# Fused H3 convolution and Infini-attention: bound products in four column tiles, a first butterfly on VectorE for two channel blocks, two loads on another queue, and a new stored order

## The chip, the cores and the metric

The kernel runs on one NeuronCore of a Trainium2 chip. A core has five engines that run side by side: TensorE (PE, matrix products into PSUM), ScalarE (ACT), VectorE (DVE), GpSimd (POOL) and SyncE (SP), the last used here only to issue DMAs. Each works through its own instructions in order; semaphores hold an instruction until what it needs is done. The metric is device time in microseconds of one execution. Before the change the median of seven runs is 310.45 us (308.61 to 312.26).

## The reference

Two independent computations are set beside each other in the last axis of the output, [1, 2048, 1280] in bf16. S = 2048, D = 640, H = 32 heads of 20.

```python
# A: long convolution (H3)
k_shift = sum over t of k shifted down by t rows * shift_k[:, t]     # t = 0..3
kv = k_shift * v
y  = irfft(rfft(kv, 2S) * rfft(ssm_k, 2S))[:S]                     # causal convolution over S
A  = q * (y + kv * ssm_D)
# B: segment attention with a memory (N = 4 segments of L = 512, per head)
for s in range(N):
    p = softmax(qs @ ks.T * scale + causal_mask)
    a_mem = (phi(qs) @ M) / (phi(qs) @ z + 1e-6)                   # phi(t) = t+1 if t > 0 else exp(t)
    o_s = g * a_mem + (1 - g) * (p @ vs)                           # g = sigmoid(beta)
    M += phi(ks).T @ vs;  z += sum(phi(ks))
B = concat(o_s) @ wo                                               # q, k, v = x @ wq, x @ wk, x @ wv
out = concatenate([A, B], -1)
```

## The kernel before

**Part A** goes through five blocks of 128 channels (`dp` 0 to 4). For each block the transform of length 4096 is split into four residues of time (`c` = 0..3), each a product with a cosine and sine table. Stages, in `a_chunks`:
- `load_kv` brings v (`vt`, four DMAs of 128 KB) and k transposed (`kr`); `load_sk` brings ssm_k and transposes it to `kT`; `load_q` brings q. For block 0 v is issued on ScalarE's queue, for the others on GpSimd's.
- `kshift(b)` forms the shifted k as 16 small products into a PSUM bank, and VectorE multiplies it with v in place (`vt<-w,vt`).
- `fwd(kind, c)` multiplies `vt` (kind "X") or `kT` (kind "K") with the table `Wf` into two banks, and ScalarE copies each to `F`.
- `bfly(kind)` combines the four residues on VectorE into `Xh` or `Kh`.
- `pointwise`, `ybfly` multiply the spectra (`S`) and combine them back, and `inverse(c)` makes four output tiles with the table `Wi`, multiplied with q by VectorE (`outa`) and stored by a DMA on GpSimd's queue.

A residue transform has eight products of 128x256. When a kind is in `SUMMED` (before: "X" for every block), `fwd` computes for c = 0..3 the sums and differences of two residues at once, by accumulating 16 products instead of eight, the difference with a negated table `Wfn`. `bfly` then skips its first two VectorE operations, one addition and one subtraction of [128, 2048].

**Part B** has eight units, u = 2 s + half: a segment s and a half of 16 heads. `proj(t)` projects k, q and v for 128 tokens (15 products of 128x320, three copies by ScalarE), and a DMA transpose on SP brings k and q to `KQT` with the head dimension on partitions, 32 partitions a head. `bound` finds for every query an upper bound of its scores, so that the softmax needs no maximum: VectorE takes the largest absolute value of each k dimension (`kam`, 128x2048 to 128x4), multiplies a selection table by it (`A`), takes |q| (`qabs`), and TensorE sums over a head's 20 dimensions. Four products, one for each group g of four heads, accumulate in 16 rows of one bank; ScalarE copies them to `bT`, and four small DMAs on SP put them into row 20 of each head's block in `KQT`, where k has ones. `mem` updates the memory. `attn(g)` makes scores for four heads at once in four row tiles, always in the one buffer `st` of four PSUM banks; ScalarE exponentiates them to `ET`, TensorE multiplies with v and the memory, and VectorE normalises. `outt` and `outproj` project to the output.

All other products use the four banks "w". The pool of banks, the tile buffers (most exist once, so the next user waits for the last reader) and the data dependencies are tracked by a recorder. Operations are first recorded, in program order, then emitted in the order that `ORDER` lists, a compressed list of operation numbers. That order alone decides how the parts A and B are interleaved on each engine and each DMA queue. DMAs issued on SP, ScalarE and GpSimd queue behind each other per issuer. Line 216 is the emission, so nearly every instruction in the profile has that line: groups are told apart by tile names.

The identity (`ident`, 32 KB) turns x into `xT` for the first segment and builds `skd`; before the change it is the second DMA of ScalarE's queue, behind x.

Of the kernel before, what the change touches and what calls it, by code (L numbers as in the profile page):

```python
# [12 lines left out]
BF16_NP = ml_dtypes.bfloat16  # L13
bf16 = mybir.dt.bfloat16
f32 = mybir.dt.float32
i16 = mybir.dt.int16
ALU = mybir.AluOpType
# [4 lines left out]
S = 2048; D = 640; C = 512; P = 1024  # L22
# [21 lines left out]
def small_consts():  # L44
    p = np.arange(128)
    d = p % 32
    hl = p // 32
    sel = np.zeros((128, 4, 16), np.float32)
    for g in range(4):
        ok = d < DH  # L50
        sel[p[ok], g, 4 * hl[ok] + g] = -1.0
    maskbd = np.zeros((128, 4, VW), np.float32)
    epsrow = np.zeros((128, 4), np.float32)
    for hh in range(4):
        rows = (hl == hh) & (d < DH)
        maskbd[rows, hh, 0:DH + 1] = 1.0
        epsrow[32 * hh + DH + 1, hh] = EPS
    later = np.zeros((128, 5, 128), np.float32)
    for b in range(4):
        later[:, b] = np.where(np.arange(128)[None, :] <= 32 * b + p[:, None] % 32, 0.0, -1e9)  # L60
    later[p, 4, p % 32] = 1.0
    return sel.astype(BF16_NP), maskbd.astype(BF16_NP), epsrow, later.astype(BF16_NP)
# [213 lines left out]
class K3:  # L276
    def __init__(self, ctx, tc, A_q, A_k, A_v, A_shift_k, A_ssm_k, A_ssm_D, B_x, B_wq, B_wk, B_wv, B_wo, B_beta, out):
# [48 lines left out]
        }  # L326
        self.skw = c.tile([128, 5, 4], bf16, name="skw")
        nc.gpsimd.dma_start(out=self.skw[:], in_=self.shift_k.rearrange("(c p) t -> p c t", p=128))
        self.ident = const("ident", np.eye(128).astype(BF16_NP), bf16, nc.scalar)
        bt = self.bt = c.tile([128, H], bf16, name="bt")  # L330
        nc.gpsimd.dma_start(out=bt[:], in_=B_beta.partition_broadcast(128))
        self.sel = const("sel", sel_np, bf16)
# [48 lines left out]
    def a_chunks(self, dp):  # L381
# [16 lines left out]
        def load_kv():  # L398
            vt = st["vt"] = self.ring("vt", [128, 4, 4, 128])
            for b in range(4):  # L400
                (nc.gpsimd if dp else nc.scalar).dma_start(out=vt[:, b], in_=self.v[512 * b:512 * b + 512, dsl].rearrange("(p c) d -> p c d", c=4))
            kr = st["kr"] = self.ring("kr", [128, 1, 4, KPAD + 512])
            nc.gpsimd.memset(kr[:, 0, :, 0:KPAD], 0.0)
            for c in range(4):
                nc.sync.dma_start_transpose(out=kr[:, 0, c, KPAD:KPAD + 512], in_=self.k[:, dsl].rearrange("(r c) d -> r d c", c=4)[:, :, c])
            w1 = st["skd"] = self.ring("skd", [128, 4, 128])[:]
            V.tensor_tensor(out=w1, in0=self.ident[:, None, :].to_broadcast([128, 4, 128]), in1=self.skw[:, dp, :, None].to_broadcast([128, 4, 128]), op=ALU.mult)
# [18 lines left out]
        def fwd(kind, c):  # L426
            def f():
                if c == 0:
                    st["F"] = self.ring("F", [128, 4, 2, 512])
                F = st["F"]  # L430
                terms = [(c, Wf[:, :, c, :])]
                if kind in SUMMED:
                    p = c % 2
                    terms = [(p, Wf[:, :, p, :]), (p + 2, (Wf[:, :, p + 2, :], self.Wfn[:, :, p, :])[c // 2])]
                for i in range(2):
                    pf = self.bank("w")
                    for j in range(2):
                        o = pf[:, 256 * j:256 * j + 256]
                        last = kind == "K" and i == 0 and terms[0][0] == 0
                        mms = [(w[:, h, 256 * i + 128 * j:256 * i + 128 * j + 128], st["vt"][:, h:4:2, cc, :] if kind == "X" else st["kT"][:, cc, h:4:2, :])  # L440
                               for cc, w in terms for h in range(2)]
                        for n, (w, rhs) in enumerate(mms):
                            nc.tensor.matmul(o, lhsT=w, rhs=rhs, start=(n == 0), stop=(n == len(mms) - 1 and not last))
                        if last:
                            nc.tensor.matmul(pf[:, 256 * j:256 * j + 128], lhsT=self.ones[0:1, :], rhs=st["Drow"][:], start=False, stop=True)
                    nc.scalar.copy(out=F[:, c, i, :], in_=pf)
            return f

        def bfly(kind):
            def f():  # L450
                F = st["F"]
                X = st[kind] = self.ring(kind + "h", [128, 8, 512])
                T = F[:, 0:2]
                if kind not in SUMMED:
                    T = X[:, 1:8:2, :].rearrange("p (c i) r -> p c i r", c=2)
                    V.tensor_tensor(out=T, in0=F[:, 0:2], in1=F[:, 2:4], op=ALU.add)
                    V.tensor_tensor(out=F[:, 2:4], in0=F[:, 0:2], in1=F[:, 2:4], op=ALU.subtract)
# [62 lines left out]
    def b_proj_chunks(self, u):  # L520
# [43 lines left out]
        def bound():  # L564
            kam = self.ring("kam", [128, 4], f32)
            V.tensor_reduce(out=kam[:], in_=KQT[:, 0:4, :], axis=AX.X, op=ALU.max, apply_absolute_value=True)
            A = self.ring("A", [128, 4, 16])
            V.tensor_tensor(out=A[:], in0=self.sel[:], in1=kam[:, :, None].to_broadcast([128, 4, 16]), op=ALU.mult)
            if s > 0:
                nc.scalar.activation(out=PqT[:], in_=QT, func=ACTF.Exp)  # L570
                tq = self.ring("tq", [128, 4, L])
# [3 lines left out]
            V.tensor_scalar(out=qabs[:].bitcast(i16), in0=QT.bitcast(i16), scalar1=0x7fff, scalar2=None, op0=ALU.bitwise_and)  # L575
            pb = self.bank("w")
            for g in range(4):
                nc.tensor.matmul(pb[0:16, :], lhsT=A[:, g, :], rhs=qabs[:, g, :], start=(g == 0), stop=(g == 3))
            bT = self.ring("bT", [16, L])
            nc.scalar.copy(out=bT[:], in_=pb[0:16, :])  # L580
            for hl in range(4):
                r = 32 * hl + DH
                nc.sync.dma_start(out=KQT[r:r + 1, 4:8, :], in_=bT[4 * hl:4 * hl + 4, :])

        def mem():
            src, dst = self.Mbd[half][s % 2], self.Mbd[half][(s + 1) % 2]
# [101 lines left out]


BANKS = {"st": (1, 2048), "w": (4, 512)}  # L690
SUMMED = ("X",)
ORDER = (
    'c-jTQ0{|FQ6a~<G-@AXdZQHhO+qT)v8f&)g)lgdvHP*b^YPP+aJ13G6iI5Ok5DAW0h=C}GhNy@DASNOrpaKlh5g9^Ei)xWAw#7zV#6dKRZkdo7Q7n$duvnHDDJ_*Hw-grNQXw7^SX_%|'
    'nJtMWwPY3_=`4$7w7izpGFdiDiPT7M8LTSOBB!N8LQ8FFERp4~+?L<cT4Kv%`K*BDvNXtmLRQ#{SUF38@>ao;pqKTwtjKN!EeCQUAM&H34YZ<G+=^Kt<U(!~K~WUOSSx@bRuJPX53->='
    '@**jQ*>D?b$xs=UP!Uzo$NE|sl(3RE-ul@@%Z@=d*hX1@D~94Ii4quXlWe+uWixGpl|?y}vC>w`%Gv-MVbxFr-&$#mv2Uz8zP3762enWW=}{N8F~w$}6zbXxn`+Z+q}{X0cE_gRu6<|s'
    'Z5pOxI;vPzYlTK=jY`%Sm8}h0pe<UW8LC-zn`Jeu2^v^aG_(e&X${dFEvz0|+82Y@$1AI6_3e|*wOW=DwQaV|vpLot9ncOB?4d2Q<+j4++eA#pc6^O)_y$`s39qf0HMh^!$llljYh??q'
    'wLP-N*1;azTkD9G)(f4{2|X|ybI``xT1R_soopta*<xE{OKhoqhbGq4Uf4@(XYK7<^u{bi^v>4B<|2}Jwf7d;qxd}ZL?67s2m5H-@Xp+y;W?svay-QjJV6Sqv9-1oE3wL!VHH-}a?Hm9'
    'tiW2-^mVolwS2v8u*SX^du*e{^(Bxu@r788Zr0uQ+BRE*MTqV3JdSU&%@*Gic<>(9(>7rv`l25q_<C%>7R2=a7>EJbZci+sSNDCE$p5t(zTckOe-_oF`Hz;&lXzlJ>O1im578C((FG6i'
    '2yqyT-9i7!_QQNHe#Fn%VLPp%e~(7~vmL}Qb_hdozz$kkkKyV3KfFUM-;F(Zji0a&Z?MIFKypvvL-7)?u+?_q7aYK0r1Vt&y`}fJ$lyQNA^R8ge3$)--FDd8`bU7j+9$MgvbBFkcmK_5'
    'u&y7mFBpNNcFa<H4{zgX{J3@X+Ws3h;|Px7DC&D{jzj}*=`H+(owQay2%SAP>v%WM;q5)6=k%VQ$+LNL@94d}lXvjUJ{Vm*i}&@@$nFt148L10Z|dhPBKvr5Z|1%In4h-lJnny3EuONP'  # L700
    'JmDw(ycP9gKG4tDSsRXi-rq<0Xdj2d9*KE8uMhG8KG=tNJ|E-xy@*F<887QY{dYg*!@QvX;iGX1<1q$f{eu62LVn5r^vizQ%Xx9X<t6+tFYmX#g5PlCd9Ua<eYk(+BYlLQ^D7>g_k5C<'
    '^oxGYvwA7N>ZSd<pFshi?3Mh9SN5mwyzkTfk<ak=c<dkWouBc)eU{Jkv;L2N>*5`M;Z^)B&f$SS^r~LXqw)gI<07IkunH@2EH2n_Ou+A`%&M%$Q8<BK{0b*A&hPqo&#gRq=6O|I&pn@J'
    '`vjlkFTI5R^#-iN|NM==^|?OJ=ld&f$Y`v~iJpjw`Oc&By%$w6t@e0K!+K1?HJ+9!xz-zTo!94UZ_GdO!9RL@e(md>`o{l)$u-5N`Uc<V3w)FRgU!Chr375)30X*sJQ<TS6|YzlrsfqC'
    'RuRSIRV$;U?9FL@3F(-g8F<rf*(Zm-ctLIDXWzoo+RRPt%f)`(F4~{=m(^AsU9uat#LH``SI{zV!lsO)xLWSb*qr$ll#zd<tTHnO%V~vI(@J0ETRjuEc`jZ?1XWZ`wPPg}P%TAN2i`;{'
    'Mp9(mLUq;9HnwL+Mp0+(^s1__?Os<=RZp=LTha8l{bQ9?Mah*yO_h_;6+?}64R_FjC3P1~)J)gWTrIRoJAAXYYK!8j4O_7fZ`)N|v&&XW@zs{C*^){1y(dsIwNyg=;H{KW+muRe)mm-T'
    'PC1yHiIiBowOt!|59^toS$PB5xQ<zPnj5&54YWrY^pmGnM(t1<?bI$cR33I=Or=#<?(=lYqOAH^gP2JJxL1Sui!v)O^YI7nVty860TyL9CQ*8I=Rp3bt{TFl>Zae+kH>UG{n=dy)I-^H'
    'Q2TXKL)lqf^sBP#dws<L`avT&P^Yw=IaGu>l}m-$lRMZ`JK0O$v$y)FpLTPvkLDhp*6%u_zB;Qy{6qcqqmSVr4dX}-(O`|@2o2{*MGPSfRirRV5yEK22*Wg7V>yB2IgXQfPUrQL_Gyfc'
    'Yn;X^W;mhA`dZ@^EtKR0O;jmPWDkC&GmIX-(IM^fVw|F>I>^J??b9?}e=2IYs0;c_aYAuUXKC*D+t}lmG((qFo-_5WCh0p>;57cNL;Oc^L;R2+lwrJZMae>va8<LFINVm!kUZQ`s!*0w'
    'IfFC#6A$w@|CLAlu72Y+-P1l^*Ac$bYwhKaOdG!CEZ)#f&C)rh4&O0dNFOqU+5Fj`>3|>QVV|S9dai^1i~s8PwVx05K*#tqU+ASOataUmS(e~re#5U>j*s*U5AY<@gva`wPc(;(bW3x2'
    'oF|wuWD40r=8!dH37_>v|L{6*@CvW;z5Zf*E#wD%R0l2M8@<&ZT)>X%q<{6Fo@zc%@e(idldkb^W)C^SO(I+*L$UBDZ?Sl=;9(vW&hr9q^Dgi39wUdGAxg*<5{6izP)HPFhr(eA^M({5'  # L710
    'cSsrXgyk#}?(+ekaVhhK{NbHea1~dxXeb{_gp%PYONG+mISYh>p-gzemwd%HtPpC1nqjfZhH_zvmTH;isbW~5%Ar!2uUesYSg0yt4UhUmuH+*w*JCc@6E4zXu2-E<H&hMP!fU=|^-wRY'
    'Q2nq{4MM}vDE!M+TC3Gsrw#g#ANZb)LzD24U)VG>3&B1S7Qx<ejW()zXc^2}g%-iBO=uT7hR&gFXdgb4);dHqS+~$BbO>ESkI+5z3|&L7@IM_MqKp'
)


# [73 lines left out]
```

## Time and profile before

| | before |
|---|---|
| median of 7 runs | 310.45 us |
| profiled execution | 312.21 us, of which span 310.4 us |
| granted TensorE clock, mean | 0.981 |
| longest VectorE rows | S (20 of 128x2048) 24.2 us, S<-Xh,Kh 22.8 us, o<-w,rr 19.7 us |
| longest ScalarE rows | ET (64 of 128x2048) 121.2 us, F 45.6 us, ET (32 of 128x1024) 33.1 us |
| longest TensorE rows | w<-wqkv,xT 78.2 us, w<-Va,ET 43.2 us, w<-vt,Wf 35.3 us |
| bound products w<-tq,A | 32 of 128x512, 8.2 us |

A row of the profile gives the engine, the operation, the tiles written and read, shapes and number, then the busy time in all, the mean duration of one in ns, and the idle time of the engine just before with what ended it. The name `tq` stands for |q| too, since both share a buffer. TensorE's products overlap, so their mean duration is longer than the time from one start to the next. The chain of waits goes back from the last instruction to what released each; its shares are shares of the span.

### The profile page before, as it was taken

What the parts mean: (1) busy time and instruction counts of PE and PEld (TensorE: products, weight loads), DVE (VectorE), ACT (ScalarE), POOL (GpSimd) and SP (SyncE); (2) the same over time, 40 slices, a digit from 0 to 9 for tenths busy, and PEclk for the clock granted to TensorE, in tenths of its full rate; (3) what the DMA queues carried; (4) which work ended last, traced back from release to release, by engine and by line L of the source; (5) the groups of instructions that cost most, each with busy time, mean ns of one, the idle gap of its engine ahead of it and who ended that gap; (6) DMA issues with size and microseconds to landing.
All of it is one profiled execution on the core that took longest, in us unless ns stands there. A gap on an engine that the chain in (4) does not pass through costs nothing.

```text
span 310.4 us, 11766 instructions
## 1 busy us (share of the span) xinstructions
PE 286.8 (92%) x5182; PEld 209.0 (67%) x5182; DVE 251.9 (81%) x382; ACT 259.1 (83%) x347; POOL 64.6 (21%) x106
## 2 busy tenths in 40 slices
PE   0889999999999999999999999999999998979694
PEld 1557777777678777767687776777676667555472
DVE  1255745998997889899989799899989999999950
ACT  1367699989998999999979999999979999976513
POOL 8100003300620000009401026200041060044233
PEclk9999999999999999999999999999999999996979
DMA  7799596557950496495536787870057850012453
GB/s 255 217 204 228 119 139 122 152 116 207 241 139 20 85 136 86 86 182 142 155 68 137 110 156 171 171 103 4 19 131 117 120 127 10 3 45 86 113 121 118
DMA packets 87347, 38.49 MB, mean 124 GB/s; under 512 B 78001, under 2 KB 84193, under 8 KB 87169
## 3 DMA queue, kind: packets, MB, share of 16 engines
q1 hardware_dynamic: 77056, 21.98, 41.3%
q0 software_dynamic: 4400, 12.28, 14.2%
q10 hardware_dynamic: 5840, 3.49, 3.8%
q8 instruction: 40, 0.66, 0.9%
q14 instruction: 11, 0.08, 0.1%
HBM read 14.15 MB, written 5.24 MB: 62 GB/s over the span
## 4 chain that ended last, share of the span: by engine, by line
PE 62%; DVE 16%; ACT 10%; issue 6%; POOL 2%; DMA 2%; POOLq 0%; ACTq 0%; DVEq 0%
PE w L216 53%; PE st L216 9%; ACT ET L216 7%; DVE S L216 6%; POOL out_dram L216 2%; DMA ident<-c_ident 2%; DVE Kh L216 1%; DVE outa L216 1%; DVE Xh L216 1%; DVE vt L216 1%; DVE o L216 1%; ACT F L216 1%; DVE pr L216 1%; DVE kam L216 1%; ACT Va L216 1%
## 5 line engine op out<-in xcount | busy, mean ns | idle before, releaser
L216 ACT ACTIVATE ET<-st 128x2048 bf16<-128x2048 f32 (+1 forms) x96 | 154.3, 1607 | 11.3 <-PE st L216 10.0
L216 PE MATMUL w<-wqkv,xT 128*128 128x320 bf16 x480 | 78.2, 307 | 1.1 <-DVE xT L216 1.1
L216 PEld LDWEIGHTS <-xT 128*128 128x128 bf16 x480 | 44.4, 100 | 23.3 <-issue 4.6
L216 ACT CAST F<-w 128x512 bf16<-128x512 f32 x80 | 45.6, 606 | 1.8 <-PE w L216 1.2
L216 PEld LDWEIGHTS <-ET 128*128 128x128 bf16 x1280 | 40.8, 96 | 6.7 <-issue 4.6
L216 PE MATMUL w<-Va,ET 128*128 128x21 bf16 x1280 | 43.2, 172 | 0.3 <-DVE outa L216 0.3
L216 PEld LDWEIGHTS <-Wf 128*128 128x128 bf16 x400 | 35.9, 97 | 10.6 <-issue 4.8
L216 DVE TENSOR_TENSOR S<-S 128x2048 bf16<-128x2048 bf16 (+1 forms) x40 | 37.6, 950 | 0.4
L216 POOL DMA_DIRECT2D vt<-in_A_v_dram x16 | 12.3, 774 | 112.7 <-PE w L216 109.8
L216 PE MATMUL w<-vt,Wf 128*128 128x256 bf16 x240 | 35.3, 273 | 0.2 <-DVE vt L216 0.2
L216 ACT CAST KQ<-w 128x320 bf16<-128x320 f32 x64 | 26.4, 438 | 10.1 <-PE w L216 9.6
L216 PE MATMUL st<-KQT 21*128 21x512 bf16 (+3 forms) x512 | 34.3, 296 | 0.0
L216 PEld LDWEIGHTS <-later 32*128 32x128 bf16 x1536 | 18.6, 92 | 22.1 <-issue 19.8
L216 PE MATMUL st<-later 32*128 32x32 bf16 (+1 forms) x1536 | 26.9, 180 | 4.9 <-ACT ET L216 4.1
L216 PE MATMUL w<-wo,oT 128*128 128x320 bf16 x160 | 27.6, 317 | 1.9 <-DVE o L216 1.9
L216 POOL DMA_DIRECT2D out_dram<-outa x20 | 15.9, 794 | 62.3 <-DVE outa L216 59.7
L216 DVE TENSOR_REDUCE kam<-KQT 128x4 f32<-128x2048 bf16 x8 | 18.2, 2280 | 10.4 <-issue 7.4
L216 PE MATMUL w<-kT,Wf 128*128 128x256 bf16 x160 | 23.4, 273 | 0.4 <-DVE o L216 0.4
L216 PE MATMUL w<-S,Wi 128*128 128x256 bf16 x160 | 22.0, 287 | 1.7 <-DVE S L216 1.4
L216 DVE TENSOR_TENSOR S<-Xh,Kh 128x4096 bf16<-128x4096 bf16 x10 | 22.8, 2284 | 0.1
L216 ACT CAST outb<-w 128x320 bf16<-128x320 f32 x32 | 13.3, 440 | 11.4 <-PE w L216 11.2
L216 PEld LDWEIGHTS <-oT 128*128 128x128 bf16 x160 | 15.6, 102 | 9.6 <-issue 3.7
(73 smaller groups left out, 418.5 us busy)
## 6 DMA issues: line engine op xcount, KB each, us to landing
qd<-in_A_q_dram POOLq DMA_DIRECT2D x20, 128.0 KB, 3.3
out_dram<-outa POOLq DMA_DIRECT2D x20, 128.0 KB, 3.0
out_dram<-outb POOLq DMA_DIRECT2D x16, 160.0 KB, 2.6
vt<-in_A_v_dram POOLq DMA_DIRECT2D x16, 128.0 KB, 3.6
kT<-in_A_ssm_k_dram POOLq DMA_DIRECT2D x4, 512.0 KB, 4.1
Wf<-c_wf ACTq DMA_DIRECT2D x4, 256.0 KB
Wi<-c_wi SPq DMA_DIRECT2D x1, 1024.0 KB
wo<-in_B_wo_dram SPq DMA_DIRECT2D x1, 800.0 KB
```

Of the source, the lines that this page charges most:

```text
L216: f(*fargs, **fkw)
```

## The change

1. `SUMMED` names kind and block: X of blocks 2, 3 and 4. For blocks 0 and 1 `fwd` makes single residues with eight products each, and `bfly("X")` does its first addition and subtraction on VectorE, as K's always did.
2. `bound`: each of the four products writes its own 32 partitions of the bank (`tile_position` (0, 32 g)), with no accumulation over g. The selection table has the same 32 columns for every g, `A` is 128x4x32, ScalarE copies all 128 rows, and each of the four DMAs reads four rows, 32 partitions apart.
3. The identity's DMA goes from ScalarE's queue to the front of SP's; v of block 0 goes from ScalarE's queue to SP's.
4. A new stored order.

```diff
-    sel = np.zeros((128, 4, 16), np.float32)
-    for g in range(4):
-        ok = d < DH
-        sel[p[ok], g, 4 * hl[ok] + g] = -1.0
+    sel = np.zeros((128, 32), np.float32)
+    ok = d < DH
+    sel[p[ok], hl[ok]] = -1.0
...
-        self.ident = const("ident", np.eye(128).astype(BF16_NP), bf16, nc.scalar)
+        self.ident = const("ident", np.eye(128).astype(BF16_NP), bf16, nc.sync)
...
-                (nc.gpsimd if dp else nc.scalar).dma_start(out=vt[:, b], in_=self.v[512 * b:512 * b + 512, dsl].rearrange("(p c) d -> p c d", c=4))
+                (nc.gpsimd if dp else nc.sync).dma_start(out=vt[:, b], in_=self.v[512 * b:512 * b + 512, dsl].rearrange("(p c) d -> p c d", c=4))
...
-                if kind in SUMMED:
+                if (kind, dp) in SUMMED:
                     p = c % 2
                     terms = [(p, Wf[:, :, p, :]), (p + 2, (Wf[:, :, p + 2, :], self.Wfn[:, :, p, :])[c // 2])]
...
-                if kind not in SUMMED:
+                if (kind, dp) not in SUMMED:
                     T = X[:, 1:8:2, :].rearrange("p (c i) r -> p c i r", c=2)
                     V.tensor_tensor(out=T, in0=F[:, 0:2], in1=F[:, 2:4], op=ALU.add)
                     V.tensor_tensor(out=F[:, 2:4], in0=F[:, 0:2], in1=F[:, 2:4], op=ALU.subtract)
...
-            A = self.ring("A", [128, 4, 16])
-            V.tensor_tensor(out=A[:], in0=self.sel[:], in1=kam[:, :, None].to_broadcast([128, 4, 16]), op=ALU.mult)
+            A = self.ring("A", [128, 4, 32])
+            V.tensor_tensor(out=A[:], in0=self.sel[:, None, :].to_broadcast([128, 4, 32]), in1=kam[:, :, None].to_broadcast([128, 4, 32]), op=ALU.mult)
...
-                nc.tensor.matmul(pb[0:16, :], lhsT=A[:, g, :], rhs=qabs[:, g, :], start=(g == 0), stop=(g == 3))
-            bT = self.ring("bT", [16, L])
-            nc.scalar.copy(out=bT[:], in_=pb[0:16, :])
+                nc.tensor.matmul(pb[32 * g:32 * g + 32, :], lhsT=A[:, g, :], rhs=qabs[:, g, :], start=True, stop=True, tile_position=(0, 32 * g), skip_group_check=True)
+            bT = self.ring("bT", [128, L])
+            nc.scalar.copy(out=bT[:], in_=pb)
...
-                nc.sync.dma_start(out=KQT[r:r + 1, 4:8, :], in_=bT[4 * hl:4 * hl + 4, :])
+                nc.sync.dma_start(out=KQT[r:r + 1, 4:8, :], in_=bT[hl:hl + 97:32, :])
...
-SUMMED = ("X",)
+SUMMED = (("X", 2), ("X", 3), ("X", 4))
```

The stored order, `ORDER`, is replaced as a whole. Decoded, it lists 1393 operations before and 1397 after; the four more are the additions and subtractions of point 1.

More of the change, by code (lines that the diff above doesn't have):

```diff
@@ L690 @@
 BANKS = {"st": (1, 2048), "w": (4, 512)}
-SUMMED = ("X",)
+SUMMED = (("X", 2), ("X", 3), ("X", 4))
 ORDER = (
[L693 to L712, printed above, removed]
@@ new lines @@
+    'c-jTQ0{|FQ6a~<C-@SjfZQHhO+xFJHW*cFs*+!Uc){GizsIA%T99Slc<}zBa7#7K*m{}H!Y!xh)MYL!Z-J)6qi)n6|Evv=%xE|YMdIFE`aXgVFw0M@-;#dri<?%eRC-JzJ-E(+CPvj{)'
+    'wdeP=p4HQN8c*q|ypUz{*p|r)TRux=`K_Smv0Rqi3wcT_;JGccXYsU_$8&mmFJeh7sb%!sp4W1D1}|#aEV~u39G24xT58Md`Mj#dw=|Z)ihD6H;pwcH74{<D-@o?ZKEV6=S6<XhdMPjM'
+    'Nj;fQ@Jc?yC;CXQ>{YykRrR5sz>---D{qypiVgNkR?f;=8JptYdKsVUWqpp%@*)16SMc&)(aZTHALWyMwh#1gypGkfVP4$E`B)$CgM744_ZdFZ=XqV5>oqLB)wcOw)2ewjt8UAEg_pE3'
+    '{=HB0hhEA`+e%;H8SO`3<v;jr``2gMKR&~z+bpZ@^{j!{w}#%vT3HioVYR%iwYHX4+Z$OktKm(pu{AgFoj0(W{@y3qG@ESQY>G{_ZMM*x_#$uW4XuvXb!RJY?f>~3f9v1cV{hY6ysgi%'
@@ new lines @@
+    'cGlj$vyN8JUwM6h>975Zcd)14$mdxH|K1vVC!24d{Tu6S#>nhqbFG~>^XA^(yLd-mW((|*FZLy#!j}0`f8mkX)t6fjCwux2Ccd&h*2z123-4+zy_a?K?*5~#vZ##Cg%*u5xY~PpZPw))'
+    'U+d58ldrZqT<5)gjXm@AzSin-gFpA?jLD7u!Xh#@TQDJ4*e2iYD=i9p+fUZV`&wV`XNee}n|+HXW&$Q*a{I-e+e=$yOKgw-<W0HQmRc;XvkkW1HriLV**4kFo|Jp6hjq7~t*8BJPwc5Z'
+    'vd8wH#X~bD<9`3(shE-}n4AYZaIbB*2;A%Y{G)%gw|2k|+AsdAAM_)3)DC$@zP3*mm+x$V^|v@Y?D2TS-`GCeWrr*icUx+1^~1K`23i^pviCOBhFMyEuyovE9l6ajbGz^GotA}-*onve'
+    'gbO3BJ&$^09<$@tgaKP^l(k_8j<;jpkab{)f|CxkWjmg*oqp1G`2;&{r>r}>aftQcV2h7a?jWL~C)2Y&PkV2k@eJ(6JnX}>e$E@PFSD{g^RhFuu`65iG{53+-j7|Fi!GU(W9+;QV0Px<'
@@ new lines @@
+    'KyI<GZLAHqA<W0$_&f9SEYI+=N5d75j#ezmi(Y`|S&EnZ0*kU3|6oDh=bt?932}}W{CBU1LHyl@au^HoYYt{%*2e=D=UtZIaE|2#8^?Pb!3wO%&-TSGb0kM|6vwbMuk!{gu?!=iG9%&{'
+    'tMCag+9k`$@tnXIxXQ9D$1A+X%k~$q+7&Cps;tI4e9GsX$Vt4-+IYxUtc&W5gqw_vzgdGd856M)3;*$&-QpacwFDSvHBcRAY@%KDb5;$%*$AtNTIh$-_6_svAHLut{>!Pn$Z0H~m%PM+'
+    '`kr%{2x*WOkNKL3@hzJm13t1muiFiK!=`x0TKtZMlo2VA5{)pK4KR=M*${8p7z_9Vr|<)tAsLcm9ZPFHZ&?zQQBrK+MmEPMzUNQ)%-i-O<6t_2BIpZEYdC}HP*O8Fi+|c578h$-O6jqX'
+    'w|x^+VKWzTF;nA?Z{b!h;WfYE_k1a@`+fhzmvK3(s<Nsnq9Uo7s>rn!(iT8eQ6*49tzZlM?NOBpUm-KHU?q!dHdk>QOQ@n&Gb^&ACF-gRy5X)zQ)FdB1$9L|bw?CcS0~h0VMSL1bw&*p'
@@ new lines @@
+    'Q4HO)o0boiR9ks*-)gCjTA?*!DxUtbSo+&yD~=kfyau4AHe(xp<yJM;Pu#4ZxlQqvNH@KS8Y!`Ec@q6&ZO~k;^sl8>OC?oXq)|I`z+LN)zx<9pus?kh9@++ML=LRO1+2#}Y^`K!s^n^;'
+    '7HW@<$b<Zds{-hOp2(uC+Rk6pR)_Vg+9`)}s;myGoQ~*_vgs!c#Xe@&e(vDU8ite_h_A5&gD@PqluCoKMIF^i?bSg$m0Ky)8wF7qJF!PYkXC!u3we}ReNYHRkWR<7OQ)1xJ(WSbbwH=p'
+    'OTQwcGHDb}Xf#ghoO-K|#$i0RtGjlnhelu*qK1*ktfDB6d}^lcD2Wm%hTZ6kXkoC1Xb<~pFVCx=e$!X#uK~KCi@K!WHBe&^C&UduBXal!gESUV!cZO6Wqqw-I;OF@qH)@%;o8al8m$SK'
+    'gozlTkvgNqp)AH|ns)K54loyTBPSmCZjRDLOh!3O#T3j&k}zGdLc&lAr7>Pd5IZCa6EsmXG)YG>Qxz~-Q#1z^F-w&(Ti10>H*{5(5i=wR$-^8~!7SX=Eu{#l!Z%7CQigQlTYaZLbc`o>'
@@ new lines @@
+    'n1AZFj`Ilb=on7&I3DOP{i6doh`*IFOw~8|7T@bTe2=-Br%d6l?kRnki_Bpk-slt#;jRAFY3#>Coxnk!#9<ub9_+<$$PzMybGU^U${OyWvtDW%s^Szcp$y7nCT5@#j&eF4={~ZB|MWNR'
+    'AbZFWa)t$(uUuh1x~QwVX&x5f49?;QEW~Zx#VbA56D`7P{RIz;@l?-r9>3#9JlB0O+`u2WhU@sOFM6jxaRu*n6*uugA7ueyDdL6rA$L$n6GF%n(uVw@Kv<@{VY%{!)p&q^@DTrE8CKwv'
+    '9^pSk2ob|eyueC4$1A)>sZcs34GUE)BnyjFJp7>O;YY;?B|^ziFf37_uvCjxIIO`N6bTi>YOPeIutuv?Ig|+-v`$sRMy*%XP&QNx)kB?7Bh(G`!dtw<dwjqb6b<D<&F~quLS%o8r&z1y'
+    'Sc_+Pf+bj?O<ILWp?vs+C|)7d4pF^+Xb>8PMuFZq$eV<wp;`C{b9e*~9?>It^UyN12(3fg&?dAC-9y*VKDc)Z9YT-LEp!eYL(kA9v<kgKpU^w>4gJFZQum~4'
```

## The prediction

> **What bounds the kernel now.** I read the page's engine shares first, then its chain of waits, then busy time by stage, then TensorE's order of time.
>
> ```profile
> PE 286.8 (92%) x5182; PEld 209.0 (67%) x5182; DVE 251.9 (81%) x382; ACT 259.1 (83%) x347; POOL 64.6 (21%) x106
> ...
> PE 62%; DVE 16%; ACT 10%; issue 6%; POOL 2%; DMA 2%; POOLq 0%; ACTq 0%; DVEq 0%
> ...
> L216 PE MATMUL w<-vt,Wf 128*128 128x256 bf16 x240 | 35.3, 273 | 0.2 <-DVE vt L216 0.2
> L216 DVE TENSOR_REDUCE kam<-KQT 128x4 f32<-128x2048 bf16 x8 | 18.2, 2280 | 10.4 <-issue 7.4
> ```
>
> TensorE (PE) is busiest and owns 62% of the chain. Its busy time alone does not prove that it paces the kernel, because one product's 273 ns hides short gaps. The stages say more:
>
> ```profile
> core 0: us, PE busy (x) PEld busy (x) DVE busy (x) ACT busy (x) POOL busy (x), PEclk, DMA share, GB/s
> ...
> 10.00:40.00 30.00, 28.30 (x252) 20.05 (x253) 15.85 (x37) 17.81 (x41) 0.00 (x0) 1.00 0.86 174
> 40.00:240.00 200.00, 197.58 (x3860) 145.99 (x3858) 176.66 (x266) 189.43 (x244) 37.60 (x56) 1.00 0.63 123
> 240.00:290.00 50.00, 45.00 (x944) 31.37 (x943) 47.35 (x64) 44.43 (x49) 12.19 (x17) 0.93 0.33 68
> 290.00:310.40 20.40, 13.58 (x114) 9.44 (x112) 9.28 (x14) 5.05 (x13) 7.06 (x11) 0.89 0.48 121
> ```
>
> From 40 to 240 us PE has 2.4 us of visible idle, ScalarE (ACT) 10.6, VectorE (DVE) 23.3. So PE paces this stretch, but ACT is already at 94.7%: that is the ceiling close above it. The reader should see that removing PE time here pays only until ACT is full. TensorE's order of time gives the prices:
>
> ```profile
> 228.69 0.39 PE L216 MATMUL w<-vt,Wf 128*128 128x256 bf16 x2
> 228.92 0.38 PE L216 MATMUL w<-vt,Wfn 128*128 128x256 bf16 x2
> 229.14 0.38 PE L216 MATMUL w<-vt,Wf 128*128 128x256 bf16 x2
> 229.36 0.38 PE L216 MATMUL w<-vt,Wfn 128*128 128x256 bf16 x2
> 229.57 0.25 PE L216 MATMUL w<-Va,ET 128*128 128x21 bf16 x4
> ...
> 237.47 0.38 PE L216 MATMUL st<-KQT 21*128 21x512 bf16 x4
> 237.79 1.26 PE L216 MATMUL w<-vt,Wf 128*128 128x256 bf16 x10
> ...
> 253.03 1.03 PE L216 MATMUL w<-tq,A 128*16 128x512 bf16 x4
> 254.00 0.27 PE L216 MATMUL st<-later 32*128 32x32 bf16 x16
> ```
>
> Start to start, eight transform products take 0.88 us, 0.110 each. Four bound products take 0.97 us, one after another. Four score products of the same 512 columns, in four row tiles, take 0.32 us: they run side by side.
>
> **What the Trainium skill says.** "Perfetto Trace Analysis", Identifying the Most-Contended Engine: matmul busy share is a bad measure of PE's headroom. The trace agrees (0.273 us a product, 0.110 apart), so I price by starts. "TensorE: Matmul & The Clock Gate", Measured speedup vs the span model: packing in column tiles runs about as fast as in row tiles (three column tiles 2.38 times, four row tiles 3.07 times). The trace has row tiles only (0.97 against 0.32, 3.0 times); column tiles are not shown here. "TensorEngine Tiling (Array Packing)", Key Properties: a change of tiling mode drains the engine. In the trace the row-tiled group at 237.36 starts 0.64 us after the last four projection products, against 4 x 0.138 = 0.55 without a stop, so about 0.1 us at most per switch.
>
> **The change part by part.**
>
> *Fewer transform products.* For channel blocks 0 and 1, v's forward transform no longer sums two terms in PSUM: 32 products a block instead of 64. 64 x 0.110 = 7.0 us of PE goes. The PSUM evacuations by ACT stay (8 copies of [128,512] a block).
>
> *First butterfly on VectorE.* Two more operations per block, [128,2048] bf16. The same pair in K's butterfly takes 1.22 and 1.21 us (rows Kh<-F and F<-F): 4 x 1.21 = 4.9 us of DVE. The sum goes into the odd rows of X's buffer, which exists once, so block 1's sum now waits until block 0's pointwise products have read X. The six butterfly operations after it had the same wait. F is held longer, and a copy to F waiting at ACT's head would hold ET behind it. Cost here between 0 (other ACT work stands between, as now: ACT's copies to F wait 0.2 us on DVE in all) and 2 x 2.4 us; I take 0.
>
> *Bound in four column tiles.* 8 groups fall from 0.97 us to between 0.32 (as row tiles) and 1.17 (serial, plus two switches): -5.2 to +1.6 us. I take -5.2, for the row tiles' sake. A doubles to 128 elements: from skd (512 elements 0.68) and A (64 in 0.22), 1.0 ns an element, so +0.07 each, 0.5 in all on DVE. The copy bT goes from 0.57 to F's 0.61: 0.3 us of ACT. The four row DMAs keep their sizes and number.
>
> *Start.* The identity lands 5.7 us after its issue at 1.25, just after x (6.6 us). Issued first on SP (SyncE, idle then) it lands by about 6.4, so x ends that wait: 0.4 us. The two weight loads behind it move up by its 0.52 us on ACT's queue, sk on SP back by as much (its consumer is needed at 15 us, not at 6). xT's evictions are reordered so that DVE takes the first bank finished, not the third: its three copies (1.89 us, ending 10.37) start about 0.5 us earlier. Together 0.9 us on the path. Idle PE time of 10 to 40 (projections waiting for Va, 1.7 us visible) is filled by K transforms that the new order puts earlier; I count 0.5.
>
> *v of block 0 on SP.* ACT's queue loses four issues of 0.55 us; SP gains them between DMA transposes of 1.25 to 1.9 us. All four stand before the first bound's row DMAs; three follow a transpose that waits for the second unit's projections. Before, v was issued from 27.6 to 35.6 us and used at 37.9; SP has 20 us of issues between 14 and 35. Covered by the projections of the second unit; uncovered, the four issues cost 2.3 us of delay to the bound's rows.
>
> *New order.* Decoded and set beside the recorded operations (1393 before, 1397 after), it is another arrangement throughout. Three places: block 0's sum and difference now precede the first attention reciprocal on VectorE, where it sat 7.39 us idle ahead of kam (42.4 to 49.8); the second unit's last three KQ transposes stand together in SP's queue, where three other transposes stood between them before; and of the last block's four output tiles two are computed before the last score's products, so less VectorE work follows them. I count 0.3 for the last.
>
> **The sum.** PE loses 7.0 + 5.2 = 12.2 us; of that 7.0 and six bound groups (3.9) lie in 40 to 240. Paced by PE alone this stretch would be 189.1 us, below ACT's 189.43 of work, so ACT ends up pacing. ACT reached 94.7% here and 10.00 in its best 10 us slices; with PE ahead of it, its 10 us of waiting for scores shrinks. At 97.5% the stretch is 189.43 / 0.975 = 194.3: 5.7 saved. At 95.75% (its share from 50 to 130, 76.60 of 80) 2.2; at 100% 10.6. With start 0.9 + 0.5, end 0.3, and 0.4 off 240 to 290, where DVE is at 95% and two bound groups lie: 7.8; I keep 0.8 back for DVE, which rises to 176.7 + 5.3 = 182 of 194 (94%). Gain 7.0. The profiled execution was 312.21 us (span 310.4 and 1.8 around it), 0.6% above the median of 310.45. So 305.2 for a profile like that, **303.5** as a median.
>
> **Rivals.**
> 1. *All the PE time comes out* (12.2): 298.3. For it: PE's idle is small everywhere. Against: ACT at 100% for 190 us.
> 2. *ACT or another wait has the place already*: 2.2 in the stretch and 1.4 at the start, less 2 to 4 for DVE: about 310. For it: ACT's 94.7%.
> 3. *Column tiles do not overlap* (the change does not do what it says): PE loses 7.0 less 1.6 at worst; ACT is no longer full, about 4 us less: 306.5.
> 4. *VectorE takes over*, the other side. Place: 50 to 130 us, where DVE has 72.42 of 80 us (90.5%) and gets 4.9. If it can't rise above that share there, the stretch becomes 77.3 / 0.905 = 85.4 us, and PE waits for VectorE's evictions with its shorter work: none of the gain, 310.45 + 5.4 = 316. It decides from where DVE's idle time there stays above 2.7 us (77.3 of 80). For it: DVE executes in order and its operations wait for PE and ACT in turn. Against: 240 to 290, where DVE did 94.7%, and the 7.39 us hole just before.
>
> **How the numbers follow.** Forecast 0.44, rival 1 0.12, rival 2 0.13, rival 3 0.08, rival 4 0.23. A difference under 0.5% (1.55 us) can't be told from none here. Faster: 0.44 + 0.12 + 0.08 and a little of rival 2, 0.65; same 0.11; slower 0.24. The forecast's own range is 300 to 307.5 (ACT at 96 to 99%). For 8 in 10 I leave out the far end of rival 1 and half of rival 4: 297.5 to 316.
>
> **What would show it.** Products w<-vt down from 320 to 256; bound groups 0.3 us apart, not 0.97; the first projection near 9.5 us, not 10.42; ACT at 97% or more of 40 to 235 with fewer waits on scores; DVE busy about 257. Wrong, if PE shows new waits on VectorE's o, vt or S between 50 and 130, if ACT's share stays at 95%, or if kam or the scores wait for SP's transposes around 40 us.

## The result, and the profile after

The changed kernel takes 1.0055 times the time before, 95% interval 1.003 to 1.008: slower by about half a per cent (1.7 us), where 7 us less were forecast. Its 27 runs scatter from 309.4 to 319.2 us (median 314.89), those of before from 308.6 to 312.4 (median of all runs 310.55); the ratio compares of each kernel only the runs within 1.5% of its fastest, over all runs the medians stand 1.4% apart, and the profiled execution shown below, 317.98 us with a span of 316.2, is one of the long ones, so that its waits are read for their place and not for their sum.

The page, first the engine shares and then the chain of waits:

```profile
PE 282.4 (89%) x5118; PEld 205.0 (65%) x5118; DVE 254.0 (80%) x386; ACT 258.7 (82%) x347; POOL 64.2 (20%) x106
...
PE 47%; ACT 17%; DVE 16%; DMA 11%; issue 6%; POOL 1%; SPq 0%; POOLq 0%; ACTq 0%; DVEq 0%
...
L215 PE MATMUL w<-skd,kr 128*128 128x128 bf16 x320 | 23.6, 233 | 5.5 <-DMA kr<-in_A_k_dram 4.8
```

The 64 products are gone (5182 to 5118), and ScalarE's work is what it was. PE's share of the chain fell from 62% to 47%. In its place stand ScalarE, which rose from 10% to 17%, and DMA, from 2% to 11%. The products of the shifted k (`w<-skd,kr`), which waited for nothing before, now wait 4.8 us for the transposed k. Busy time by stage shows where:

```profile
core 0: us, PE busy (x) PEld busy (x) DVE busy (x) ACT busy (x) POOL busy (x), PEclk, DMA share, GB/s
40.00:50.00 10.00, 8.52 (x170) 5.89 (x169) 6.44 (x11) 9.59 (x14) 1.46 (x3) 1.00 0.72 121
50.00:60.00 10.00, 6.41 (x85) 4.24 (x82) 4.44 (x7) 5.03 (x7) 5.67 (x9) 0.77 1.06 160
60.00:70.00 10.00, 9.39 (x229) 7.58 (x230) 8.41 (x17) 8.16 (x11) 0.00 (x0) 0.89 0.69 155
70.00:140.00 70.00, 67.53 (x1360) 49.87 (x1360) 67.95 (x100) 69.09 (x91) 7.23 (x12) 1.00 0.69 120
140.00:150.00 10.00, 8.53 (x119) 5.57 (x118) 7.69 (x14) 8.69 (x14) 7.27 (x11) 0.88 1.06 208
```

From 50 to 60 us VectorE and ScalarE stand half idle and TensorE for more than a third, and the granted clock drops to 0.77. From 70 to 140 us ScalarE is busy 69.09 of 70 us: what it lost before that it can't catch up. A second, smaller hole follows at 140 to 150; there block 3's products wait 1.5 us for k. TensorE's order of time around the first, and SyncE's queue ahead of it:

```profile
50.82 1.53 PE L215 MATMUL w<-wqkv,xT 128*128 128x320 bf16 x10
52.32 0.23 PE L215 MATMUL w<-skd,kr 128*128 128x128 bf16 x1
55.88 1.78 PE L215 MATMUL w<-skd,kr 128*128 128x128 bf16 x15 [3.34 <-DMA kr<-in_A_k_dram]
...
44.79 2.13 SPq L215 DMA_TRANSPOSE xT<-in_B_x_dram  x1
47.01 3.83 SPq L215 DMA_TRANSPOSE kr<-in_A_k_dram  x3
50.89 1.27 SPq L215 DMA_TRANSPOSE xT<-in_B_x_dram  x1
```

Block 1's shifted k is asked for at 52.3 us, its last transposes were issued between 47.0 and 50.8, and one lands only at 55.9. In the old order the same transposes were issued from 48.7 to 53.6, and TensorE asked for k at 60.4, some 7 us later:

```profile
48.74 4.82 SPq L216 DMA_TRANSPOSE kr<-in_A_k_dram  x3
...
60.40 1.07 PE L216 MATMUL w<-skd,kr 128*128 128x128 bf16 x16
```

So the transposes moved forward by 3 us and their reader by 8. With block 3 it is the other way round. Its products stand at 145.6 us (145.8 before), but the last transpose of its k is issued at 140.1 us instead of 123.3.

Of two parts of the change one does as the prediction said and one does so in part. The bound's four products run side by side:

```profile
48.28 0.40 PE L215 MATMUL w<-tq,A 128*32 128x512 bf16 x4
48.65 0.27 PE L215 MATMUL st<-later 32*128 32x32 bf16 x16
```

From the group to the next instruction it is 0.37 us, 0.97 before. And x's first products start at 5.15 us instead of 7.00, since they no longer wait for the identity; but the last four of them then wait 1.53 us for a bank that VectorE has to copy first, and the first projection starts at 9.95, 0.5 us earlier than before and not 0.9. VectorE is late because a copy of ssm_k (`kT`, 1.23 us) stands ahead of x's copies in its order. The load of ssm_k, now behind the identity on SyncE's queue, lands at 6.7 us instead of 5.0.

### The profile page after: what moved, and what is told of

Read it like the earlier page. It is cut to its first block, busy times and chain, and to the rows that moved or that the text cites. A ratio compares the mean times of both kernels' runs of the same rounds, so it can differ in the third digit from the quotient of the medians.

```text
span 316.2 us, 11617 instructions
## 1 busy us (share of the span) xinstructions
PE 282.4 (89%) x5118; PEld 205.0 (65%) x5118; DVE 254.0 (80%) x386; ACT 258.7 (82%) x347; POOL 64.2 (20%) x106
## 4 chain that ended last, share of the span: by engine, by line
PE 47%; ACT 17%; DVE 16%; DMA 11%; issue 6%; POOL 1%; SPq 0%; POOLq 0%; ACTq 0%; DVEq 0%
PE w L215 41%; ACT ET L215 8%; DVE S L215 6%; PE st L215 6%; DMA kr<-in_A_k_dram 4%; ACT F L215 4%; DVE o L215 2%; DMA kT<-in_A_ssm_k_dram 2%; DMA Wf<-c_wf 2%; ACT KQ L215 2%; DMA xT<-in_B_x_dram 2%; ACT PqT L215 1%; DVE pr L215 1%; DMA oT<-o_s 1%; DVE Kh L215 1%
## 5 line engine op out<-in xcount | busy, mean ns | idle before, releaser
L215 ACT ACTIVATE ET<-st 128x2048 bf16<-128x2048 f32 (+1 forms) x96 | 155.9, 1624 | 18.7 <-PE st L215 16.7
L215 ACT CAST F<-w 128x512 bf16<-128x512 f32 x80 | 48.0, 627 | 4.1 <-PE w L215 3.2
L215 PEld LDWEIGHTS <-Wf 128*128 128x128 bf16 x368 | 33.3, 98 | 12.1 <-issue 5.3
L215 PE MATMUL st<-KQT 21*128 21x256 bf16 (+3 forms) x512 | 34.8, 300 | 0.0
L215 ACT CAST KQ<-w 128x320 bf16<-128x320 f32 x64 | 27.5, 452 | 7.9 <-PE w L215 7.6
L215 PE MATMUL w<-vt,Wf 128*128 128x256 bf16 x208 | 29.8, 273 | 1.3 <-ACT F L215 1.1
L215 PE MATMUL w<-skd,kr 128*128 128x128 bf16 x320 | 23.6, 233 | 5.5 <-DMA kr<-in_A_k_dram 4.8
L215 PEld LDWEIGHTS <-kr 128*128 128x128 bf16 x320 | 20.8, 105 | 8.6 <-DMA kr<-in_A_k_dram 5.4
L215 PE MATMUL w<-kT,Wf 128*128 128x256 bf16 x160 | 24.6, 281 | 1.7 <-DMA Wf<-c_wf 0.7
L215 POOL DMA_DIRECT2D qd<-in_A_q_dram x20 | 15.0, 754 | 44.4 <-DVE outa L215 44.4
```

Source lines behind the costliest of these rows:

```text
L215: f(*fargs, **fkw)
```

## The experiments

Each time is a ratio to the kernel before on the same chip, with its 95% interval. 1% is 3.1 us.

### The code edits apart, in the old order

Three kernels are made from the kernel before, with its stored order kept: the column tiles alone, the unsummed X of blocks 0 and 1 alone, and all edits of the code.

```diff
# b_cols: sel, A, the four products, bT and its DMAs as in the change, nothing else
+nc.tensor.matmul(pb[32 * g:32 * g + 32, :], ..., tile_position=(0, 32 * g), ...)
# b_unsum: SUMMED as in the change; the addition and subtraction directly ahead of
# each block's butterfly in the order, whose four operations run with X's even rows first
+SUMMED = (("X", 2), ("X", 3), ("X", 4))
# b_all: both, with the identity and v of block 0 on SyncE's queue
```

> The kernel before with the bound in four column tiles alone, everything else and the old stored order kept. Theory 1 (the code edits are sound, the new order's late DMAs cost the time): each bound group takes 0.37 us instead of 0.97 on TensorE, 8 x 0.6 = 4.8 us less, of which ScalarE's ceiling lets through part: 307 to 310 us. Theory 2 (the edits themselves cost): 310.5 us or more, with new waits on bT or A.

> The kernel before with X of blocks 0 and 1 not summed, the old order kept, the addition and subtraction put just ahead of each block's butterfly. Theory 1: TensorE loses 7.0 us, VectorE gains 4.9, of which 2.4 fall beside its old idle time at 42 to 50 us: 306 to 310. Theory 2 (VectorE takes over): 312 to 316, VectorE above 95% from 50 to 130 us with TensorE waiting for o, vt or S.

> All code edits (column tiles, no sums in blocks 0 and 1, identity and v of block 0 on SyncE's queue) in the old order. Theory 1: no hole at 50 to 60 us, 303 to 308. Theory 2: as slow as the changed kernel or slower, 312 to 316.

Measured: column tiles 0.9939 (0.9917 to 0.9961), unsummed 1.0141 (1.0106 to 1.0177), all edits 1.0125 (1.0082 to 1.0168). So the column tiles gain 1.9 us, and the exchange of products for VectorE operations costs 4.4. The two together would give 1.0079; the 0.5% left for the queues is within what the intervals allow. The times of theory 2 hold for the exchange, and not for the column tiles. Its sign, VectorE above 95% from 50 to 130 us, does not show: with all edits VectorE is busy there 72.45 of 80 us, 72.42 before.

### What the exchange consists of

One kernel takes only the products away, one only adds the VectorE operations.

```diff
# b_pecut, in fwd: X of blocks 0 and 1 single residues, bfly unchanged
-                if kind in SUMMED:
+                if kind in SUMMED and dp > 1:
# b_dummy, in bfly: all products kept, two operations whose result is overwritten
+                if kind == "X" and dp < 2:
+                    for op in (ALU.add, ALU.subtract):
+                        V.tensor_tensor(out=X[:, 1:8:2, :].rearrange("p (c i) r -> p c i r", c=2), in0=F[:, 0:2], in1=F[:, 2:4], op=op)
```

> The kernel before with the transform products of X halved in blocks 0 and 1 and nothing added on VectorE: the additions and subtractions of residues are left out, so the values of part A differ there. TensorE loses 7.0 us, ScalarE and VectorE do what they did. If TensorE paces those stretches (the prediction), 304 to 306 us. If VectorE or the loop of scores and exponentials does (what the last runs hint at), 309 to 311.

> The kernel before with two extra VectorE operations of [128,2048] at the place of block 0's and block 1's butterfly, their results overwritten, and no product taken away: 4.9 us more on VectorE alone. If VectorE's time there lies on the path and the saved products are worth nothing, the time equals that of the unsummed kernel, 314 to 316 us. If the saved products give something back, it is slower than that, 317 or more. If VectorE has room, 310 to 312.

Measured: without the products 1.0028 (1.0002 to 1.0053), with the dummies 1.0141 (1.0098 to 1.0184). The dummies cost what the exchange costs, and 7.0 us of TensorE time at these places are worth nothing: at 312.1 us in the median the kernel without the products lies a little above even the second of its ranges. Busy time by stage without the products:

```profile
core 0: us, PE busy (x) PEld busy (x) DVE busy (x) ACT busy (x) POOL busy (x), PEclk, DMA share, GB/s
40.00:50.00 10.00, 7.44 (x170) 5.54 (x167) 2.70 (x5) 9.51 (x14) 0.00 (x0) 1.00 0.89 145
50.00:90.00 40.00, 36.60 (x735) 25.74 (x732) 38.23 (x58) 38.16 (x51) 11.46 (x18) 1.00 0.73 172
```

In these 50 us TensorE is busy 44.0 us, against 49.4 in the kernel before (9.87, 9.80, 9.77 and 20.00). VectorE has 40.9 both times, ScalarE 47.7 both times. TensorE simply waits longer. For what, the chains in order of time say at the place behind block 0's products, first of the kernel before, then without the products:

```profile
50.60 2.34 PE w L216 x18
52.94 0.45 PE st L216 x24
...
50.92 2.04 ACT ET L216
52.96 0.04 issue
53.00 0.52 PE st L216 x24
```

Before, TensorE's own work reaches the scores (`st`) at 52.94 us. Without the products the exponential of ScalarE releases them, at 53.00. The same happens behind block 1's products, at 80.21 and 80.11. The chain names one path, and a second one ended within a tenth of a microsecond of it.

For VectorE's operations the kernel before's chain shows this at block 0's butterfly:

```profile
55.53 0.52 DVE xm L216
56.08 0.23 DVE xm L216
56.31 0.84 DVE tq L216
57.16 0.59 DVE Xh L216
57.75 0.26 DVE Mbd L216
58.01 1.13 DVE pr L216
59.14 1.21 DVE Xh L216 x2
60.38 1.14 DVE S L216
```

With pauses of 0.03 us at most between them, VectorE is the chain from 55.5 to 61.5 us, and goes on to 68.2 with one long pause, of 1.07 us, behind this. Two of these pieces belong to block 0's butterfly (`Xh`). With the dummies the same piece of the chain reads:

```profile
54.14 1.24 DVE Xh L216
55.40 3.03 DVE Xh L216 x4
...
59.66 0.60 DVE Xh L216
```

The two operations stand at its front, and what follows is the same, from here on 2.5 us later. At block 1 the chain of the kernel before would have misled. There it runs on TensorE alone, from 68.2 to 106.9 us, and with the dummies it runs on VectorE:

```profile
80.67 2.55 PE w L216 x14
83.22 0.32 PE st L216 x20
...
83.76 1.14 DVE Xh L216
84.92 2.43 DVE Xh L216 x3
```

The first two lines are the kernel before. VectorE was nearly as full there, 18.96 of 20 us from 70 to 90 beside TensorE's 20.00, so that two more operations put it ahead.

The starts of VectorE's reciprocals, one to each attention step, follow this through the kernels of the old order (us, difference to before; from the orders of time). The columns are the kernels b_cols, b_pecut, b_dummy and b_all; K4 is b_best, of which more below:

```
step (segment, half, group)  before | cols  pecut  dummy  all    K4
0, 0, 1                       63.2  | -0.6  -0.2   +2.5   +3.2   -0.7
0, 1, 2                       91.3  | -0.6  +0.2   +4.9   +6.6   -0.6
1, 0, 3                      134.3  | -1.1  +0.2   +3.8   +5.7   -1.0
2, 0, 3                      206.5  | -1.6  +0.6   +3.8   +5.3   -1.4
3, 0, 3                      264.3  | -1.9  +0.6   +3.8   +4.9   +1.0
3, 1, 3 (the last)           291.4  | -2.9  +0.7   +3.8   +4.1   +0.6
```

The dummies add 2.5 us at block 0 and 2.4 at block 1, the two operations' duration each time; 1.1 of it is made up soon after, and from 134 us on the difference is constant to a tenth of a microsecond.

### The new order: what it hides and what it adds

If VectorE's operations lay on the path in the new order as well, summing X of all blocks again would gain. This undoes the exchange as a whole, so the 64 products come back too. If v on SyncE's queue held up the transposes, moving it back would gain.

```diff
# a_sum: the four VectorE operations dropped from the new order, the 64 products back
+SUMMED = tuple(("X", dp) for dp in range(5))
# a_vact: the identity and v of block 0 back on ScalarE's queue, new order
```

> The changed kernel with X of all blocks summed again, the four VectorE operations dropped from the new order and the rest kept. If the VectorE operations lie on the path in the new order too, 307 to 310 us. If the new order's late transposes of k are the whole loss, the hole at 53 to 58 us stays and the time is 311 to 315.

> The changed kernel with the identity and v of block 0 back on ScalarE's queue, in the new order. Theory 3 (v on SyncE's queue holds up the transposes behind it): the four issues of 0.56 us leave SyncE's queue, k of block 1 lands 2 us earlier, 308 to 311. Theory 1: the hole at 53 to 58 us stays, 311 to 316.

Measured: 1.0135 (1.0069 to 1.0201) and 1.0134 (1.0075 to 1.0193). Neither is faster than the change's 1.0055; by the medians of all runs they take 2.1% and 1.7% more than the kernel before, the change 1.4%. In the new order the exchange costs nothing that undoing it would give back. Whether its operations are hidden there or paid for by its products, this doesn't separate. Both expectations had the hole at 53 to 58 us stay if k were the cause, and in neither profile does it. The last of block 1's k is issued by 50.2 and 49.8 us (50.8 in the change), and its products start at 53.3 and 53.6 without a wait. Block 3's wait longer instead, 2.6 and 2.8 us where the change has 1.5. As the first wait is gone in a_sum too, where v stays on SyncE's queue, v's queue is not shown to be its cause, and taking v back doesn't make the kernel faster. Four kernels try to bring k earlier, or to ask for it later:

```diff
# a_dma: in the order, wo behind the bound rows of segment 1's first half,
#        q of block 0 (four DMAs) behind v of block 2
# a_krfirst: in the order, k of block 1 (four transposes) ahead of x of segment 1 (four)
# a_late, a_late15: the order put off by 30 or 15 places for block 1's shifted k up to
#        the copies of its spectrum, and block 3's shifted k; dependences and banks kept
+    late = {("A", dp, stage) for dp in (1, 3) for stage in (range(1, 9) if dp == 1 else range(1, 5))}
+    order = put_off(rec, list(order), late, 30)
```

> The changed kernel with the output weights (800 KB) and the four loads of q for block 0 moved behind the second block's loads, so that they leave the DMA engines free while k of block 1 is transposed. If they delay the transposes, k lands 2 us sooner, the hole at 53 to 58 us shrinks from 5.0 to under 3 us of idle ScalarE, and the time is 308 to 312. If the transposes are simply issued too late, nothing changes: 311 to 316.

> The changed kernel with the four transposes of k for block 1 ahead of the four of x for the second segment on SyncE's queue. Late k is the wait at 52 to 56 us: k lands about 5 us sooner. If only its place in the queue matters, the hole closes and the time is 307 to 311 us. If the transposes as a whole are the limit there (eleven in 16 us), x is late in k's place, the hole moves to the projections, and the time stays at 311 to 316.

> The changed kernel with, in the stored order, the operations of block 1 from its shifted k to the copies of its spectrum, and the shifted k of block 3, put off by 30 places (some 7 us). If the new order loses only because these stand too close behind the transposes of k, the waits for k go as they did without the transposes: 305 to 310 us, and the times scatter less. If delaying them costs elsewhere what it gains, 311 to 316.

> The same, put off by 15 places (some 3.5 us, about the length of the wait for k). First theory: between the changed kernel and the last one, 307 to 312 us. Second: 311 to 316.

Measured: 1.0307 (1.0255 to 1.0359), 1.0256 (1.0211 to 1.0301), 1.0586 (1.0528 to 1.0643) and 1.0507 (1.0465 to 1.055). All are slower, and all took longer than either of their theories allowed (316 us at most). With the DMA engines cleared of the output weights and of q, the hole stays; the chain and the stages say so:

```profile
49.14 6.82 DMA kr<-in_A_k_dram
...
50.00:60.00 10.00, 6.02 (x82) 4.02 (x83) 4.43 (x7) 5.04 (x7) 2.33 (x4) 0.83 0.81 134
```

k still lands at 56.0, so these loads are not what delays it; the loads of v and ssm_k for block 1 stayed beside the transposes. What this kernel lost further is a longer wait for block 3's k, 4.4 us. Whether the moved loads cause it was not followed. With k first, x is late in its place. These are the waits of TensorE, with the total, number and longest:

```profile
PE w L215 <- DMA xT<-in_B_x_dram: 3.5, 1, 3.5
PE w L215 <- DMA kr<-in_A_k_dram: 2.9, 1, 2.9
```

The second wait is block 3's. So the eleven transposes from 36.6 to 52.2 us in the change (three of k and q, four of x, four of k) look like a limit as a whole: whether x or k comes last, what comes last is late. Asking later does not help either. With 15 places block 1's wait for k shrinks to 0.6 us, but VectorE's waits for copies of F come to 8.7 us and its waits for TensorE to 8.1 at its reciprocals. What late k costs is seen when the transposes go:

```diff
# a_nokr, b_nokr: in the new and in the old order
-            for c in range(4):
+            for c in range(4 if dp == 0 else 0):
                 nc.sync.dma_start_transpose(out=kr[:, 0, c, KPAD:KPAD + 512], ...)
```

> The changed kernel without the sixteen transposes of k for blocks 1 to 4: these blocks use the k of block 0, so part A's values differ. It shows what late k costs the new order: without it the holes at 53 to 58 and 145 to 147 us go, and the time is 303 to 308. If the new order's loss lies elsewhere, 310 to 314.

> The same left out of the kernel before (blocks 1 to 4 use the k of block 0). In the old order k's products stand some 8 us behind its transposes, so nothing waits for k: 309 to 311 us. If it gains as much as the changed kernel does, late transposes are no property of the new order.

Measured: new order 0.9956 (0.9928 to 0.9985), old order 0.9994 (0.9972 to 1.0017). The new order gains 1.0% from it (1.7% by the medians of all runs), the old one nothing. By time the new order's kernel lies between its two theories, the old order's where it was expected. The new order's stage from 50 to 60 us is full:

```profile
50.00:60.00 10.00, 9.63 (x246) 7.73 (x241) 8.73 (x17) 9.14 (x12) 4.97 (x8) 1.00 0.80 231
```

The starts of the reciprocals, now as differences to this kernel without the transposes, show where the kernels of the new order lose (us, one execution each):

```
step (segment, half, group)  a_nokr | change  a_sum  a_vact  a_dma  a_krfirst
0, 0, 0                        54.1 |  +4.9    +2.7   +1.9    +4.8   +5.0
1, 0, 3                       134.5 |  +4.7    +6.2   +2.9    +4.4   +5.1
1, 1, 1                       146.8 |  +7.9   +11.3   +8.1   +11.4   +9.4
3, 1, 3 (the last)            290.0 |  +7.8   +11.2   +8.1   +11.3   +9.4
```

All lose in the same two stretches, up to 134 us and between the steps at 134 and 147, where block 3's products wait for k, and nothing from there to the end. In a_sum the larger part of the first loss is no wait for k: TensorE stops at 61.8 us for 2.3 us, and the profile shows no reason. Only the sixteen transposes separate the change from the kernel without them; since these share SyncE's queue with those of x and of k and q, their effect on the latter is in this number too.

### What beats both

Two kernels build on the column tiles in the old order. One carries the exchange the other way, the other adds the identity's move.

> The kernel before with the four column tiles, and the opposite of the change's exchange: K of block 4 summed as well, so that two VectorE operations (2.4 us) go where the chain of waits ran on VectorE (266 to 271 us), and 32 more products (3.5 us) come where TensorE was 88% busy. If VectorE's time is what lies on the path, 306 to 308.5 us, 1 to 2 below the column tiles alone. If TensorE's is, 310 to 313.

> The kernel before with the four column tiles and the identity first on SyncE's queue, v of block 0 left on ScalarE's. Old order. The identity's earlier landing was counted as 0.4 us: 308.5 to 309.5 if so, beside 309.4 for the column tiles alone. If ssm_k, now second on that queue, or x is late instead, 309.5 to 311.

```diff
# b_best: b_cols, and K of block 4 summed (two VectorE operations less, 32 products more)
+SUMMED = tuple(("X", dp) for dp in range(5)) + (("K", 4),)
# b_colsid: b_cols, and the identity first on SyncE's queue
```

Measured: 1.0014 (0.9991 to 1.0037) and 0.9941 (0.9918 to 0.9963). The first missed its forecast. The place was chosen by the chain in order of time, which runs on VectorE from 266 to 271 us in the kernel before. But the 3.5 us of products came onto the path: at the step at 264 us K4 stands at +1.0 in the table and the column tiles at -1.9. Where VectorE had been the chain, this was now it:

```profile
252.20 3.31 PE w L215 x26
...
268.18 1.89 ACT ET L215
...
274.78 1.89 ACT ET L215
277.34 1.89 ACT ET L215
```

The chain is TensorE from 252 to 258 us, and later one exponential after another. The identity's move adds nothing to the column tiles. The fastest of all kernels here is the one before with the column tiles alone (0.9939), or with the identity as well: both are faster than the kernel before and than the change.

## Why the prediction was wrong

**The step that failed** is "So PE paces this stretch", for 40 to 240 us, and with it the term "5.7 saved". It rests on 2.4 us of visible idle. The text before it warns that a product's 273 ns hides short gaps, and then uses the same busy time to name the engine. The runs put in its place: the 7.0 us of the transforms were worth nothing (1.0028), and the bound's 4.8 were worth 1.9. Where the transform products went, ScalarE's exponential released the next scores at 53.00 us, 52.94 before. So the ceiling "close above" was there, but the room below it was about nothing and not 5.7 us. ScalarE's share of 40 to 235 us, forecast at 97% or more, was 92.4% in the execution shown. This is shown where the products of blocks 0 and 1 stand, up to 80 us. Later in the stretch only bound products were taken away, and behind it, at 252 to 258 us, 3.5 us of added products did cost time.

A second step failed too: what the new order does to the loads of k was put at nothing, and it cost 1.0% (below, under the new order).

**VectorE's added operations** were priced right, 4.9 us for four, and mis-sized on the path: 0.8 was kept back, and 4.4 is what they cost in the old order. This is rival 4's mechanism, in time (316 there, 315.1 with all edits in the old order) and in its argument: VectorE's share from 50 to 130 us did not rise (90.5% before, 90.6% with all edits). The hole of 7.39 us ahead of `kam`, which the prediction counted as room, was none in the old order: it ends at 49.8 us, and the last of the transform products that the operations need starts at 50.5. In the new order the two operations of block 0 run at 50.9 to 53.3 us, just ahead of VectorE's 4.4 us wait for the products that late k holds up.

**Bound in column tiles**: from 0.97 to 0.37 us (2.6 times as fast), priced at 0.32. The price was right, and rival 3 fell. What it is worth was not: 1.9 of the 4.8 us.

**The start**: 0.9 forecast for the identity and xT's copies, 0.5 seen at the first projection, and no effect in the time by the identity's move alone. The prediction let ssm_k come later because its consumer is needed at 15 us. Its first consumer is a copy on VectorE, ahead of x's copies.

**v of block 0 on SyncE's queue**: cost counted as covered. No gain from taking it back, though the first wait for k was gone in that profile; in the old order up to 0.5% may be its cost, not settled.

**The new order** was credited with 0.8 us in all. The exchange no longer costs 4.4 us in it, and late k puts 1.0% on. Block 1's k is asked for 8 us earlier than before and issued only 3 us earlier; block 3's is issued 17 us later, with its reader in the same place. The prediction saw three transposes change their place in SyncE's queue. It did not compare the places of the transposes of k with the place of the products that read them. It named a wait for SyncE's transposes around 40 us as what would prove it wrong, for `kam` or the scores; it was for k.

**The sum**, from the runs: -0.6% for the column tiles, +0.2% for all else without the transposes of k, and +1.0% for these make the +0.55% measured. The last two are differences of measured ratios, so the parts add up by themselves; the +0.2% says that the new order without late k does about as well as the old one with the column tiles alone. By its time (312) the result is nearest to rival 2's 310, and rival 2's mechanism, that ScalarE has the place already, is what the trial without the products shows. That the two times lie near each other is coincidence, since late k is in none of the four rivals.

What is not settled: which step of the loop of scores, exponentials and copies sets the pace from 134 to 206 us, where two of the bound's groups became 0.6 us shorter and the steps moved by 0.5 us in all; why the times of the new order scatter more, which they do without the transposes too (307.0 to 314.4); and whether an order exists that keeps the operations hidden and gives k its time. The two attempts to put the reader of k off were slower.

## What to carry to other kernels

Before an operation is traded between engines, look at the chain of waits in order of time at the place where it will stand, and do not rest on it alone. It shows one path, and others may end just behind it. Here it named TensorE for block 1, where taking products away gave nothing, and VectorE for block 4, where taking operations away in exchange for products made the kernel slower. The engine with the highest busy share may be waiting, and then its work is worth nothing. A trial that only adds the cost and one that only takes the work away price such a trade in two runs. When an order is replaced, compare for every buffer the place of its load with the place of its first reader, and count what else is queued at the issuer between them.

## What was not expected of the hardware

Transposes by DMA: with eleven issued in 15.6 us on SyncE's queue, 1.2 to 2.1 us each, one issued at 49.6 us landed at 55.9, 6.3 us later, and at 6.8 with 1.3 MB of other loads moved away. Four plain loads of 128 KB on GpSimd's queue between 30 and 60 us took 9.5 us to land in the median, where all twenty of their kind have 3.1.

A hole can cost more than its length. Behind the change's wait of 3.3 us the granted clock fell to half for 6 us (columns as in the stages above):

```profile
54.00:56.00 2.00, 0.12 (x2) 0.12 (x3) 0.00 (x0) 0.00 (x0) 1.67 (x3) 0.85 1.65 126
56.00:58.00 2.00, 2.00 (x35) 1.75 (x38) 0.24 (x1) 0.00 (x0) 0.00 (x0) 0.50 0.80 56
58.00:60.00 2.00, 2.00 (x18) 1.06 (x10) 1.75 (x5) 1.46 (x1) 0.00 (x0) 0.50 0.86 252
60.00:62.00 2.00, 2.00 (x35) 1.67 (x37) 1.16 (x3) 1.09 (x3) 0.00 (x0) 0.50 1.05 301
62.00:64.00 2.00, 2.00 (x46) 1.73 (x39) 1.32 (x4) 1.61 (x1) 0.00 (x0) 0.94 1.04 277
```

Against the kernel without the transposes the first attention step comes 4.9 us later and the second 5.9. The waits of 3.5 us in a_krfirst and 3.2 us in b_all went with 0.50 as well, a wait of 1.9 us in b_dummy did not (1.00 throughout). And the old order repeats: with the dummies all steps from 100 to 291 us stand 3.7 to 3.8 us behind.
